# A gated decode block: the last V's joining ahead of eight late w_o steps, its copy on two engines, other pieces of the last transfer

## The chip, the cores and the metric

The kernel runs on one core of one Trainium2 chip. The core has TensorE (matmuls; PE in the profile, with its weight loads as PEld), VectorE (DVE), ScalarE (ACT), GpSimd (POOL) and SyncE (SP, which here issues nearly all transfers), and 16 DMA engines that bring data from HBM into SBUF. Matmul results stand in PSUM.

The metric is the device time of one execution in microseconds. The time before is 377.09 us, the median of 3 runs (376.98 to 377.14).

## The reference

One decode step of grouped-query attention on a cache, gated by a small bilinear network, all in float32:

```python
# B = 2, Sq = 1, D = 448, Hq = 16, Hkv = 8, Sk = 4096, Dh = 256, F = 1792
def A(x, k_cache, v_cache, wq, wo):
    q = (x @ wq).reshape(B, Sq, Hq, Dh).transpose(0, 2, 1, 3)
    k = repeat(k_cache, Hq // Hkv, axis=1)
    v = repeat(v_cache, Hq // Hkv, axis=1)
    p = softmax(einsum("bhqd,bhkd->bhqk", q, k) * Dh ** -0.5)
    o = einsum("bhqk,bhkd->bhqd", p, v)
    return o.transpose(0, 2, 1, 3).reshape(B, Sq, Hq * Dh) @ wo

def G(x, w_gate, w_up, w_down):
    return ((x @ w_gate) * (x @ w_up)) @ w_down

xn = layernorm(x)
out = x + A(xn, ...) * silu(G(xn, ...))
```

The caches are most of the data: 16 pairs of a batch row and a K/V head, each with 4 MB of K and 4 MB of V. With the weights some 158.5 MB are read once.

## The kernel before, in words

**Staging.** K and V of a pair stand in SBUF as tiles of 128 partitions by 8,192 float32 columns (`ROW`). The pool `ring` has two buffers of 16,384 columns. Each holds V of one pair and K of the next (`vk`), so a buffer is free again, and SyncE may issue the next transfer into it, when the scores on its K are done. Weights pass through one buffer, `slot`. The order of all transfers is a list written out by hand (`plan`, lines 82 to 90), and `issue(n)` (line 59) hands the next n of them to SyncE at places chosen in the code. An entry can have cuts: each piece between two cuts is a transfer of its own (lines 69 and 70), in the order of the columns, and its readers wait for that piece only.

The last two entries differ from the rest. `last0` holds K of pair 15 and V of pair 14, in two pieces. `last1` (line 90) holds V of pair 15 and behind it, under the name `wo2`, those chunks of w_o that are used last. Its cuts make six pieces: V's columns in 4,096, 3,072 and 1,024, then the chunks in groups of five, four and one.

**A pair.** `scores(i)` (line 231) multiplies q with K: 16 matmuls of 512 columns in four column groups of TensorE side by side. `softmax` (line 246) takes the maximum over the pair's four groups through two small TensorE transposes and the exponential on ScalarE, and VectorE transposes the result (`pT`). `over` (line 266) sums and inverts. `values(i, pT, o, lo, hi)` (line 274) multiplies with V: blocks e from lo to hi of 512 columns each, block e in column group e % 4; the four groups add up partial sums in one PSUM bank. Of 16 blocks, 0 to 3 begin the sums and 12 to 15 end them. In the profile each float32 matmul stands as two records.

**Joining.** ScalarE copies the partial sums to SBUF (`ob`), scaled by the inverse sum. `combine` (line 281), called the joining here, adds the four groups' parts with eight small matmuls against a matrix of ones and zeros (`add_blocks`), reading `ob` and writing the bank `cb`. `turn` (line 296) is a VectorE transpose of `cb` into `oT0`, `oT1` or `oT2`, the form in which TensorE takes it as weights. Both batch rows of a K/V head land in the same `oT` tile.

**Output projection.** w_o has 32 chunks of 128 rows by 448 columns, 224 KB each; chunk i belongs to K/V head i // 4. Chunks 0 to 15 need `oT0`, 16 to 27 need `oT1`, and 28 to 31 need `oT2`, which is complete only after the last V. `project` (line 302) multiplies chunk i in column group i % 4 into the bank `wide`; it runs for chunks 0 to 15 in the middle of the kernel and for 16 to `LATE` - 1 near the end (line 353). `lift` copies `wide` to SBUF and `spread` (line 201) adds up its four groups into the bank `acc`, 112 columns to a group.

The other chunks are the late steps. `project_last` (line 308) does one with four matmuls of 112 columns straight into `acc`. Their order, which is also their order in the transfer, is the list `THIRD` (line 28): ten of them, 22 to 26, then 28 to 31, then 27.

**The end.** Each engine works through its own instructions in the program's order. After line 353 stand: the softmax of pair 15; `values` of pair 14 (line 357); `spread`; the copy of pair 14 (line 361); blocks 0 to 7 of pair 15 into `o`, which takes the bank `wide` over (line 363); the joining and turn of pair 14; blocks 8 to 15; the copy of pair 15 on ScalarE (line 367); late steps 22 to 24; the joining and turn of pair 15 (lines 370 and 371); late steps 25, 26, 28 to 31 and 27. Then VectorE multiplies `acc` with the gate and adds x (lines 380 and 381), and the result is stored.

`wo` on the host (lines 415 to 417) is put in the order of chunks 0 to `LATE` - 1 followed by `THIRD`; the first `LATE` chunks are the transfer into `slot` that is issued with the pairs in the middle, the rest is appended to the last V.

Of the kernel before, what the change touches and what calls it, by code (L numbers as in the profile page):

```python
# [9 lines left out]
AF = mybir.ActivationFunctionType  # L10
OP = mybir.AluOpType
AX = mybir.AxisListType

B, D = 2, 448
# [8 lines left out]
ROW = 8192  # L23
SL = D // NT
NC = HKV * 4
EARLY = 16
LATE = 22
THIRD = [22, 23, 24, 25, 26, 28, 29, 30, 31, 27]
PART = 28 * FC
EXTRA = 4  # L30
SIDE = 16
# [8 lines left out]
def gated_decode_block(ctx: ExitStack, tc: tile.TileContext, x, first, vk, last0, last1, wq0, wq1, wqx, wo, wgu, wd, out):  # L40
    nc = tc.nc
# [7 lines left out]
    def bank(name="s", bufs=3):  # L49
        return psum.tile([128, 512], F32, name=name, bufs=bufs)  # L50
# [4 lines left out]
    LAST = N - B  # L55
# [3 lines left out]
    def issue(n=1):  # L59
        for names, src, cuts in todo[:n]:  # L60
            weight = names[0].startswith("w")
            if weight:
                t = slot.tile([128, PART], F32, name="slot", align_bytes=512)
            else:
                t = ring.tile([128, 2 * ROW], F32, name="ring", align_bytes=512)
            width = ROW if not weight else PART // len(names)
            for i, name in enumerate(names):
                loaded[name] = t[:, i * width:(i + 1) * width]
            for lo, hi in zip(cuts, cuts[1:]):
                nc.sync.dma_start(t[:, lo:hi], src[:, lo:hi])  # L70
            if names == ["wq1"]:
                at = src.shape[1]
                loaded["wqx"] = t[:, at:at + EXTRA * 512]
                nc.gpsimd.memset(loaded["wqx"][:64], 0.0)
                for a in range(2):
                    nc.sync.dma_start(loaded["wqx"][a * 32:a * 32 + SIDE], wqx[:, a])
        del todo[:n]

    def plan(names, src, cuts=None):
        todo.append((names.split(), src, cuts or [0, src.shape[1]]))  # L80
# [6 lines left out]
        if i in weights:  # L87
            plan(*weights[i])
    plan(f"k{LAST + 1} v{LAST}", last0, [0, ROW, 2 * ROW])
    plan(f"v{LAST + 1} wo2", last1, [0, 4096, 7168, *(ROW + i * D for i in (0, 5, 9, 10))])  # L90
    issue(3)


# [41 lines left out]
    oT1 = const.tile([128, 3, 2, REP, W], F32)  # L135
# [60 lines left out]
    def lift(ps):  # L196
        t = work.tile([128, D], F32, name="h")
        nc.scalar.copy(t, ps[:, :D])
        return t
# [66 lines left out]
    def over(p):  # L266

        pT, su, sm = p
        nc.vector.tensor_add(su[:, 2:3], su[:, 0:1], su[:, 1:2])  # L269
        nc.tensor.matmul(sm[:, 130:131], add_head.rearrange("p a r j -> p (a r j)"), su[:, 2:3], start=True, stop=True)  # L270
        nc.vector.reciprocal(su[:, 3:4], sm[:, 130:131])
        return pT, su[:, 3:4]

    def values(i, pT, o, lo=0, hi=KB):

        for e in range(lo, hi):
            h, t, at = e // 8, e % NT, e % 8 * 2 * W
            nc.tensor.matmul(o[W * t:W * (t + 1), :], pT[h][:, at:at + 2 * W:2],  # L278
                             loaded[f"v{i}"][:, e * 512:(e + 1) * 512], start=e < NT, stop=e >= KB - NT)

    def combine(ob, n):

        cb = bank("cb", 1)
        src = ob.rearrange("p s (e d c k) -> p s e d c k", e=2, d=2, c=NT)
        for e in range(2):
            for c in range(NT):
                nc.tensor.matmul(cb[W * c:W * (c + 1), :n * 64], add_blocks[:, e].rearrange("p r j -> p (r j)"),  # L287
                                 src[:, :n, e, :, c, :], start=e == 0, stop=e == 1)
        return cb
# [6 lines left out]
    def turn(oT, cb, g, b, n):  # L296
        nc.vector.transpose(oT[:, g:g + n, :, :, DUP * b:DUP * (b + 1)].rearrange("p g d r j -> p (g d) r j"), cb)

    def heads(oT, i, first):
        return oT[:, i // 4 - first, i % 2, i % 4 // 2]  # L300

    def project(oT, first, lo, hi):
        for i in range(lo, hi):
            t = i % NT
            nc.tensor.matmul(wide[W * t:W * (t + 1), :D], heads(oT, i, first),  # L305
                             loaded["wo"][:, i * D:(i + 1) * D], start=i < NT, stop=i >= LATE - NT)

    def project_last(oT, first, i):
        for n in range(NT):
            at = THIRD.index(i) * D + n * SL  # L310
            nc.tensor.matmul(acc[W * n:W * (n + 1), :SL], heads(oT, i, first), loaded["wo2"][:, at:at + SL],  # L311
                             start=False, stop=i == THIRD[-1])

    query(0)
    ob = work.tile([128, 8, 512], F32, name="ob", bufs=1)
    oT0 = const.tile([128, 4, 2, REP, W], F32)
    oT2 = const.tile([128, 1, 2, REP, W], F32)
# [3 lines left out]
    for i in range(LAST):  # L321
        g, b = divmod(i, B)
        o = bank("o", 1)
# [10 lines left out]
        if i == 7:  # L334
# [3 lines left out]
            ob = work.tile([128, 8, 512], F32, name="ob", bufs=1)  # L338
# [13 lines left out]
    ps = [over(p)]  # L352
    project(oT1, 4, EARLY, LATE)
    t = lift(wide)
    p = softmax(*ss)
    o = bank("o", 1)
# [5 lines left out]
    o = bank("wide", 1)  # L362
# [1 line left out]
    cb = combine(ob[:, 6:], 1)  # L364
    turn(oT2, cb[:, :64], 0, 0, 1)
    values(LAST + 1, ps[1][0], o, KB // 2, KB)
    nc.scalar.activation(ob[:, 7], o, AF.Copy, scale=ps[1][1])
    for i in range(LATE, 25):
        project_last(oT1, 4, i)
    cb = combine(ob[:, 7:], 1)  # L370
    turn(oT2, cb[:, :64], 0, 1, 1)
    for i in range(25, 27):
        project_last(oT1, 4, i)
    for i in range(28, 32):
        project_last(oT2, 7, i)
    project_last(oT1, 4, 27)

    r0 = work.tile([128, D], F32, name="h")[:, :SL]
    r1 = work.tile([128, D], F32, name="h")[:, :SL]
# [50 lines left out]
```

## Time and profile before

| what | value |
|---|---|
| median of 3 runs | 377.09 us (376.98 to 377.14) |
| the profiled execution | 378.13 us |
| its span, first to last instruction | 376.3 us |
| mean granted TensorE clock | 0.779 |
| TensorE busy | 203.2 us (54% of the span) |
| VectorE busy | 73.1 us (19%) |
| ScalarE busy | 40.1 us (11%) |
| read from HBM | 158.54 MB, 421 GB/s over the span |
| the hardware DMA queue | 97.7% of 16 engines' span |

Times in the profile are microseconds from the start of the span unless marked ns. A line of the chain of waits has a start, a duration and what it was spent on; "DMA ring<-last" there is the time from the issue of a transfer to its landing. A line of the timeline has the start, the duration, the engine, the line of the kernel, the operation, the tile written and the tiles read, the shapes and the number of records; in brackets stand the engine's idle time before it and what ended it. In a list of transfers the last number is the median time from issue to landing. A line of the windows has the window, its length, each engine's busy time with its count of records, the granted TensorE clock, the busy share of the DMA engines and the GB/s that they moved. A group of instructions has its total busy time and the mean ns of one.

### The profile page before, as it was taken

How to read it: one execution, taken by the hardware profiler on the slowest of the kernel's cores; microseconds unless marked ns; L12 is line 12 of the kernel's file. 1: busy time of each engine (PE TensorE's matmuls, PEld its weight loads, DVE VectorE, ACT ScalarE, POOL GpSimd, SP SyncE). 2: the span in 40 equal slices, each digit the busy share in tenths (PEclk: the TensorE clock that was granted, in tenths of full speed). 3: DMA queues.
4: the chain of work that ended last, by engine and by line, in shares of the span. 5: the costliest groups of instructions: out<-in, count | busy, mean ns of one | idle time of the engine just before them, and what ended most of it. 6: DMA issues, size and time to landing. Idle time of an engine off the chain costs nothing.

```text
span 376.3 us, 3394 instructions
## 1 busy us (share of the span) xinstructions
PE 203.2 (54%) x1470; PEld 62.6 (17%) x1470; DVE 73.1 (19%) x179; ACT 40.1 (11%) x88; POOL 3.1 (1%) x8
## 2 busy tenths in 40 slices
PE   1550648091853919558282758513636372829773
PEld 1110112020210202102120212101111111213223
DVE  4012040003040030300403041300213021212510
ACT  1001020001012020100101010100102011010300
POOL 1000000000001000000000000000000000000000
PEclk9987588778678667896778689885859596859996
DMA  8998999998989999999999999999999999999992
GB/s 339 438 491 383 420 453 439 441 446 384 488 383 441 446 411 476 439 432 399 439 447 446 413 415 447 435 439 446 439 418 434 446 439 404 434 415 444 408 421 100
DMA packets 4121, 158.74 MB, mean 422 GB/s; under 512 B 490, under 2 KB 620, under 8 KB 876
## 3 DMA queue, kind: packets, MB, share of 16 engines
q1 hardware_dynamic: 4104, 158.54, 97.7%
q8 instruction: 11, 0.18, 0.2%
q14 instruction: 2, 0.02, 0.0%
q10 hardware_dynamic: 4, 0.00, 0.0%
HBM read 158.54 MB, written 0.01 MB: 421 GB/s over the span
## 4 chain that ended last, share of the span: by engine, by line
DMA 79%; PE 19%; SPq 1%; issue 0%; DVE 0%
DMA ring<-vk 67%; PE o L278 11%; PE s L241 8%; DMA ring<-last 6%; DMA ring<-first 5%; PE acc L311 1%; SPq L70 1%; DVE h L380 0%; DVE h L381 0%
## 5 line engine op out<-in xcount | busy, mean ns | idle before, releaser
L278 PE MATMUL o<-ring,pT 128*32 128x512 f32 x480 | 82.0, 846 | 83.4 <-DMA ring<-vk 82.7
L242 DVE TENSOR_REDUCE m<-s 128x1 f32<-128x512 f32 x32 | 22.1, 691 | 206.5 <-PE s L241 206.4
L241 PE MATMUL s<-ring,qT 128*32 128x512 f32 x512 | 59.7, 607 | 4.2 <-DMA ring<-first 4.2
L278 PEld LDWEIGHTS o<-ring,pT 128*32 128x32 f32 x480 | 20.3, 149 | 136.4 <-issue 109.1
L260 ACT ACTIVATE p<-s,m 128x512 f32<-128x512 f32 x32 | 21.7, 683 | 90.9 <-DVE m L255 90.9
L328 ACT ACTIVATE ob<-o,su 128x512 f32<-128x512 f32 x14 | 9.6, 688 | 196.8 <-PE o L278 196.8
L270 PE MATMUL sm<-su,add_head 128*128 128x1 f32 x32 | 8.2, 325 | 38.2 <-DVE su L269 38.2
L262 DVE STREAM_TRANSPOSE pT<-p 128x512 f32<-128x512 f32 x32 | 22.1, 711 | 15.7 <-ACT p L260 15.7
L241 PEld LDWEIGHTS s<-ring,qT 128*32 128x32 f32 x512 | 17.4, 112 | 43.3 <-issue 39.2
L176 PE MATMUL s<-slot,xnT 128*32 128x448 f32 (+1 forms) x94 | 15.3, 782 | 4.3 <-DMA slot<-wq 3.6
L270 PEld LDWEIGHTS sm<-su,add_head 128*128 128x128 f32 x32 | 6.8, 265 | 40.4 <-DVE su L269 40.3
L249 PE MATMUL sm<-ident,m 128*1 128x128 f32 x16 | 4.3, 269 | 15.1 <-DVE m L247 15.1
L251 DVE TENSOR_REDUCE mx<-sm 1x128 f32<-1x512 f32 x16 | 10.9, 678 | 8.3 <-PE sm L249 8.3
L254 PE MATMUL sm<-one,mx 1*128 1x1 f32 x16 | 3.5, 218 | 12.4 <-DVE mx L251 12.4
L305 PE MATMUL wide<-slot,oT 128*32 128x448 f32 x44 | 6.3, 681 | 0.0
L260 ACT ACTIVATION_READ_ACCUMULATOR p<-s,m 128x1 f32 x32 | 6.3, 196 | 0.0
L249 PEld LDWEIGHTS sm<-ident,m 128*1 128x1 f32 x16 | 1.3, 79 | 28.8 <-issue 23.1
L287 PE MATMUL cb<-ob,add_blocks 128*32 128x64 f32 (+2 forms) x64 | 5.9, 491 | 0.0
L176 PEld LDWEIGHTS s<-slot,xnT 128*32 128x32 f32 x94 | 3.6, 141 | 13.2 <-issue 13.2
L278 PE MATMUL wide<-ring,pT 128*32 128x512 f32 x32 | 4.2, 599 | 2.2 <-DMA ring<-last 2.2
L222 PE MATMUL s<-slot,hT 128*32 128x448 f32 x28 | 5.1, 842 | 0.0
L188 DVE STREAM_TRANSPOSE qT<-s 128x256 f32<-128x256 f32 x4 | 1.6, 428 | 17.9 <-PE s L179 17.9
(69 smaller groups left out, 55.9 us busy)
## 6 DMA issues: line engine op xcount, KB each, us to landing
ring<-last SPq DMA_DIRECT2D x2, 4096.0 KB, 19.3
slot<-wgu SPq DMA_DIRECT2D x1, 6272.0 KB
slot<-wo SPq DMA_DIRECT2D x1, 4928.0 KB, 41.4
ring<-first SPq DMA_DIRECT2D x1, 4096.0 KB, 20.4
slot<-wq SPq DMA_DIRECT2D x1, 3584.0 KB, 11.2
slot<-wq SPq DMA_DIRECT2D x1, 3328.0 KB, 33.6
slot<-wd SPq DMA_DIRECT2D x1, 3136.0 KB, 37.7
ring<-last SPq DMA_DIRECT2D x1, 2048.0 KB, 15.6
```

The costliest lines, as they stand in the source:

```text
L176: nc.tensor.matmul(ps[W * c:W * (c + 1), :n], xnT[:, k, :], block(NT * k + c), start=k == 0, stop=False)
L241: nc.tensor.matmul(s[W * c:W * (c + 1), :], q[:, d], k[:, h, d, c, :], start=d == 0, stop=d == 1)
L242: nc.vector.tensor_reduce(m[:, h:h + 1], s, axis=AX.X, op=OP.max)
L249: nc.tensor.transpose(sm[:1, :128], m[:, 2:3], ident)
L251: nc.vector.tensor_reduce(mx, sm[:1, None, :128].rearrange("p o (c j) -> p o j c", c=NT).to_broadcast([1, NT, W, NT]), axis=AX.X, op=OP.max)
L260: nc.scalar.activation(p, ss[h], AF.Exp, bias=m[:, 3:4], scale=1.0 / 16, accum_out=su[:, h:h + 1])
L262: nc.vector.transpose(t, p)
L270: nc.tensor.matmul(sm[:, 130:131], add_head.rearrange("p a r j -> p (a r j)"), su[:, 2:3], start=True, stop=True)
L278: nc.tensor.matmul(o[W * t:W * (t + 1), :], pT[h][:, at:at + 2 * W:2], loaded[f"v{i}"][:, e * 512:(e + 1) * 512], start=e < NT, stop=e >= ...
L287: nc.tensor.matmul(cb[W * c:W * (c + 1), :n * 64], add_blocks[:, e].rearrange("p r j -> p (r j)"), src[:, :n, e, :, c, :], start=e == 0, s ...
L305: nc.tensor.matmul(wide[W * t:W * (t + 1), :D], heads(oT, i, first), loaded["wo"][:, i * D:(i + 1) * D], start=i < NT, stop=i >= LATE - NT)
L328: nc.scalar.activation(ob[:, b * 4 + g if g < 4 else b * 3 + g - 4], o, AF.Copy, scale=p[1])
```

## The change

Two more chunks of w_o, 22 and 23, go with the early w_o transfer and are multiplied by `project`. Eight late steps are left: 24 to 26, 28 to 31, 27. The last transfer is cut otherwise: V in 6,144 and 2,048 columns, the late steps in groups of three, three, one and one. The copy of pair 15 is shared: ScalarE scales and copies the first 256 columns, VectorE the other 256. The joining and turn of pair 15 stand ahead of all late steps.

```diff
-LATE = 22
-THIRD = [22, 23, 24, 25, 26, 28, 29, 30, 31, 27]
+LATE = 24
+THIRD = [24, 25, 26, 28, 29, 30, 31, 27]
...
-    plan(f"v{LAST + 1} wo2", last1, [0, 4096, 7168, *(ROW + i * D for i in (0, 5, 9, 10))])
+    plan(f"v{LAST + 1} wo2", last1, [0, 6144, *(ROW + i * D for i in (0, 3, 6, 7, 8))])
...
     values(LAST + 1, ps[1][0], o, KB // 2, KB)
-    nc.scalar.activation(ob[:, 7], o, AF.Copy, scale=ps[1][1])
-    for i in range(LATE, 25):
-        project_last(oT1, 4, i)
+    nc.scalar.activation(ob[:, 7, :256], o[:, :256], AF.Copy, scale=ps[1][1])
+    nc.vector.tensor_scalar(ob[:, 7, 256:], o[:, 256:], ps[1][1], None, op0=OP.mult)
     cb = combine(ob[:, 7:], 1)
     turn(oT2, cb[:, :64], 0, 1, 1)
-    for i in range(25, 27):
-        project_last(oT1, 4, i)
-    for i in range(28, 32):
-        project_last(oT2, 7, i)
-    project_last(oT1, 4, 27)
+    for i in THIRD:
+        project_last(*((oT2, 7) if i >= 28 else (oT1, 4)), i)
```

## The prediction

> **What bounds the kernel now.** I read the chain of waits first, by engine and then in order of time.
>
> ```profile
> DMA 79%; PE 19%; SPq 1%; issue 0%; DVE 0%
> ```
>
> ```profile
> 345.46 0.33 SPq L70
> 345.84 0.42 SPq L70
> ...
> 347.26 23.51 DMA ring<-last
> ...
> 370.91 2.13 PE acc L311 x40
> ```
>
> The kernel is a stream of transfers, and the chain leaves it only at 370.77 us (347.26 + 23.51), when the piece with w_o steps 28 to 31 lands. Behind that landing stand five late steps on TensorE (40 records, 2.13 us), then two VectorE operations and the store. Only this tail can change: the bytes are the same. The issues of the last pieces and their times to landing give the schedule of the tail.
>
> ```profile
> 347.73 1.12 SPq L70 DMA_DIRECT2D ring<-last  x1
> ```
>
> ```profile
> ring<-last SPq DMA_DIRECT2D x1, 2048.0 KB, 15.6
> ring<-last SPq DMA_DIRECT2D x1, 1536.0 KB, 18.9
> ...
> ring<-last SPq DMA_DIRECT2D x1, 224.0 KB, 23.6
> ```
>
> The 2,048 KB of V landed at 345.46 + 15.6 = 361.06, the next 1,536 KB at 345.84 + 18.9 = 364.74, steps 28 to 31 at 370.77, step 27 at 347.73 + 23.6 = 371.33. So 1,536 KB take 3.68 us, 0.54 us for the 224 KB of one step (the last piece: 0.56) and 1.23 us for 1,024 columns of V. What the engines do around this is in the timeline.
>
> ```profile
> 352.65 1.70 PE L305 MATMUL wide<-slot,oT 128*32 128x448 f32 x12
> 354.27 0.27 PE L249 MATMUL sm<-ident,m 128*1 128x128 f32 x1
> 355.32 0.22 PE L254 MATMUL sm<-one,mx 1*128 1x1 f32 x1 [0.77 <-DVE mx L251]
> 356.23 3.64 PE L278 MATMUL o<-ring,pT 128*32 128x512 f32 x32 [0.70 <-DMA ring<-last]
> 359.69 0.38 PE L203 MATMUL acc<-h,add_tiles 128*32 128x112 f32 x8
> 360.00 0.38 PE L270 MATMUL sm<-su,add_head 128*128 128x1 f32 x2
> 361.18 1.93 PE L278 MATMUL wide<-ring,pT 128*32 128x512 f32 x16 [0.80 <-DMA ring<-last]
> 362.89 0.43 PE L287 MATMUL cb<-ob,add_blocks 128*32 128x64 f32 x16
> ```
>
> ```profile
> 364.76 2.30 PE L278 MATMUL wide<-ring,pT 128*32 128x512 f32 x16 [1.43 <-DMA ring<-last]
> 366.00 0.15 PEld L278 LDWEIGHTS wide<-ring,pT 128*32 128x32 f32 x4 [0.24 <-DMA ring<-last]
> 367.11 0.69 ACT L367 ACTIVATE ob<-wide,su 128x512 f32<-128x512 f32 x1 [6.47 <-PE wide L278]
> 368.66 0.78 PE L311 MATMUL acc<-ring,oT 128*32 128x112 f32 x24 [1.60 <-DMA ring<-last]
> 369.26 0.41 PE L287 MATMUL cb<-ob,add_blocks 128*32 128x64 f32 x16
> 369.74 0.25 DVE L297 STREAM_TRANSPOSE oT<-cb 128x64 f32<-128x64 f32 x1 [6.10 <-PE cb L287]
> 370.91 2.10 PE L311 MATMUL acc<-ring,oT 128*32 128x112 f32 x40 [0.85 <-DMA ring<-last]
> ```
>
> Steps 22 to 24 waited for their piece until 368.66, 0.86 us after the copy of the last V (367.11 + 0.69), and the joining (L287) stood behind them. A late step costs 0.20 us there (368.66 to 369.26 for three), but 0.4 us in the last row (2.10 over five). The windows, cut at the clock's own borders, say why; after the window and its length come the busy us of PE, PEld, DVE, ACT and POOL, then the granted clock.
>
> ```profile
> 114.49:117.90 3.41, 1.64 (x20) 0.33 (x12) 0.00 (x0) 2.08 (x3) 1.80 (x1) 1.00 1.00 428
> 117.90:121.31 3.41, 0.00 (x0) 0.00 (x0) 0.27 (x1) 0.00 (x0) 0.00 (x0) 1.00 1.02 442
> 121.31:124.73 3.42, 2.45 (x12) 0.60 (x16) 0.00 (x0) 0.00 (x0) 0.00 (x0) 0.50 0.84 364
> 124.73:128.14 3.41, 3.41 (x20) 0.79 (x16) 0.00 (x0) 0.00 (x0) 0.00 (x0) 0.50 1.24 538
> ...
> 326.12:329.53 3.41, 1.54 (x14) 0.35 (x6) 1.65 (x4) 0.00 (x0) 0.00 (x0) 1.00 0.89 384
> 329.53:332.94 3.41, 0.61 (x3) 0.50 (x2) 1.75 (x5) 1.45 (x4) 0.00 (x0) 0.50 1.02 442
> ...
> 336.36:339.77 3.41, 2.80 (x16) 0.91 (x20) 0.00 (x0) 0.00 (x0) 0.00 (x0) 0.50 1.05 452
> 339.77:343.18 3.41, 3.41 (x36) 1.05 (x32) 0.00 (x0) 0.69 (x1) 0.00 (x0) 1.00 1.07 461
> ...
> 367.08:370.49 3.41, 1.39 (x56) 1.15 (x56) 0.25 (x1) 0.69 (x1) 0.00 (x0) 1.00 0.60 244
> 370.49:373.90 3.41, 2.10 (x40) 1.73 (x40) 0.55 (x2) 0.00 (x0) 0.00 (x0) 0.50 0.02 6
> ```
>
> The clock changes only on a grid of 3.413 us (114.49 to 370.49 is 75 of them). After a stretch with 1.54 us of TensorE or less the next one is granted 0.50; with 1.64 us it stays at 1.00. From 0.50 it rises after 2.80 us and doesn't after 2.45. The wait up to 368.66 left 1.39 us in its stretch, so the five steps behind the last landing ran at half clock.
>
> **The change part by part.** *Two w_o chunks move from the last transfer into the w_o one.* 448 KB pass earlier, so everything in the stream between moves back by 448 / 1,536 x 3.68 = 1.07 us, and the end stays at 371.33. On TensorE L305 gets two steps more, 1.70 / 6 = 0.28 us each, under the wait for the last but one V. That V's 32 records then run from 357.30 instead of 356.23, and the two groups behind them end at 361.45 instead of 360.38. Late steps fall from ten to eight.
>
> *V in 6,144 and 2,048 columns, late steps in 3, 3, 1, 1.* SP issues six transfers as before. Counted back from 371.33 at 0.56 for the last step and 0.54 for the others: step 31 lands at 370.77, 28 to 30 at 370.23, 24 to 26 at 368.6, the second V piece at 367.0, the first (2 x 1.23 earlier) at 364.5. TensorE can thus begin this V at 364.55 where it began at 361.18, and has no work from 361.45 on: 3.1 us idle.
>
> *The V itself at full clock.* Eight blocks take 1.71 us (361.18 to the next group at 362.89), so 364.55 + 1.71 = 366.26; the first joining, 0.25 (a place in the row, not its 0.43 with drain), 366.5; eight blocks, 368.2; drain, 368.45. The second piece (367.0) is there when its blocks begin at 367.4.
>
> *The shared copy.* Half-width copies aren't in the trace; the nearest rows bound them.
>
> ```profile
> L227 ACT ACTIVATE h<-s 128x112 f32<-128x112 f32 x1 | 0.3, 264 | 0.0
> ...
> L367 ACT ACTIVATE ob<-wide,su 128x512 f32<-128x512 f32 x1 | 0.7, 688 | 6.5 <-PE wide L278 6.5
> ```
>
> ```profile
> L215 DVE TENSOR_TENSOR h<-s,h 128x448 f32<-128x448 f32 x1 | 0.6, 625 | 8.7 <-PE s L179 8.7
> ...
> L380 DVE TENSOR_TENSOR h<-acc,gate 128x112 f32<-128x112 f32 x1 | 0.3, 275 | 3.1 <-PE acc L311 3.1
> ```
>
> On a straight line between widths, 256 columns take 264 + 144/400 x 424 = 417 ns on ScalarE and 275 + 144/336 x 350 = 425 ns on VectorE. In the built program's order the VectorE half waits for ScalarE's semaphore, not only for TensorE's. So the halves follow each other: 0.42 + 0.43 and 0.06 between them, 0.91 us where the whole copy takes 0.69; were they side by side, 0.43. I take 0.91; 0.43 to 1.0 is the range. The second joining waits for both, and all eight late steps stand behind it on TensorE (24 to 26 will have landed at 368.6 and are held until 369.7); the two last VectorE operations wait for them.
>
> The Trainium skill ("PSUM — Partial Sum Buffer", section on bank collisions) says that two engines may not touch one bank in the same 32 partitions at once, even two readers. That speaks against a gain from sharing, as the built order does; no row here shows it.
>
> *The tail.* Copies from 368.5 to 369.4, joining from 369.47, transpose by 369.47 + 0.41 + 0.04 + 0.25 = 370.2. Steps 24 to 26 from 369.7 to 370.3 (0.20 each), 28 to 30 (landed and turned) to 370.9, 31 to 371.1. Step 27 waits for its landing, 371.33, and 0.14 until TensorE begins (as 370.77 to 370.91); its 8 records take about 0.38 (0.20 and drain): the steps end at 371.85 against 373.04. Counted by work alone they would end near 371.6, so 0.25 us of slack swallows most of the errors above. The stretches here hold over 2 us of TensorE, so the clock stays full. Sum: 1.2 us less.
>
> The profiled execution took 378.13 us, its span 376.3; the median of the runs is 377.09, 1.04 below it. I take the same saving off the median, 375.9, and add 0.1, since nearly every unknown above can only lengthen it: **376.0 us**.
>
> **The rivals.** The idle time from 361.45 to 364.55 is where they lie, because the grid's place against the kernel decides. With a border at x between 359.9 and 360.4, the stretch from x holds under 1.54 us of work, the clock halves at x + 3.41 (before 364.55), and the next stretch holds 2.2 to 2.7 us, too little to rise. *Two stretches at half clock*: V runs at half speed from 364.55 to about 370.35 and loses 2.9 us; copies, joining and eight steps follow, ending near 374.5: +1.5, **378.6 us**, slower. It decides from the point where V's blocks stand at half clock at 367.1 still. For it: the recorded grid has a border at 360.25. Against: only 0.5 of 3.41 us of places do it, and 2.53 us there lies between the 2.45 that didn't rise and the 2.80 that did.
>
> *One stretch at half clock*: with the border between 358.7 and 359.3 (or the recorded one, if 2.53 us suffices) 1.7 us are lost; V ends at 370.15, copies at 371.1, joining and eight steps (0.25 + 1.6 + 0.26) at 373.2: +0.2, **377.3 us**.
>
> In the other places, some 70%, nothing is lost. In half of all places the clock halves at 357.0 to 358.7 already, since TensorE idles before the last but one V too; its blocks then end up to 1.7 us later, at 363.1, still ahead of 364.55, and that fills the gap.
>
> The Trainium skill ("TensorE: Matmul & The Clock Gate", Part 1) has the window at 3,413 ns and free-running, and lets the clock fall after an idle one. The grid agrees. By its rule a gap of 3.1 us would never halve the clock, and both rivals would give 376.0; the rows (1.39 and 1.54 us busy, and it fell) say otherwise.
>
> *The old tail was already fast in the timed runs*: if their grid stood so that the last five steps ran at full clock, they ended at 370.91 + 1.0 + 0.2 = 372.1, and the change gains 0.25 us: **376.8 us**. For it: the profiled execution is 1.04 us above the median, about what half clock costs the five steps. Against: profiling alone may cost that.
>
> **How the numbers follow.** Forecast 0.47; fast old tail 0.12; one stretch 0.15; two stretches 0.21; the rest 0.05. The forecast's own range is 375.6 to 376.5. The range is 375.5 (sharing side by side, all steps on time) to 378.9 (two stretches and a copy of 1.0). A measurement here can tell 0.2%, 0.75 us, from no change: faster is below 376.34, slower above 377.84. Faster 0.43 (nearly all of the forecast), same 0.29 (fast old tail, one stretch, the forecast's slow end), slower 0.28 (two stretches, the rest and some of one stretch).
>
> **What would show it.** Right: V's first block at about 364.5, the last piece at 371.3, ScalarE's half of 0.42 us ending before VectorE's begins, the second joining ahead of all late steps near 369.5, one step (8 records) behind the last landing, granted clock 1.00 from 364 to the end. Wrong: the copies overlapping; a landing order other than counted; TensorE still busy with V after 368.5 at 0.50, which would make it one of the slower rivals.

## The result, and the profile after

| | median | lowest to highest | runs |
|---|---|---|---|
| before | 377.19 us | 376.87 to 378.20 | 22 |
| after | 378.28 us | 376.73 to 379.57 | 22 |

The ratio is 1.0024, with a 95% interval from 1.0013 to 1.0035: the change made the kernel slower, by 0.24% as that ratio has it and by 1.09 us from median to median.

The spread is as telling as the median. The 22 runs after fall into three groups: 4 from 376.73 to 377.16, 15 from 377.88 to 378.71, 3 from 379.40 to 379.57. Before, 18 of 22 lie between 376.87 and 377.39 and 4 between 377.88 and 378.20. Over all 106 runs of the kernel before in this study 28 are in the upper group, 26%.

The profiled execution of the changed kernel took 378.10 us (span 376.2) and so belongs to the middle group, the usual one. That of before, 378.13 us, belonged to the upper and rarer one. Side by side the two profiled executions are equal, and the loss shows only once it is seen which of their groups they come from.

First the shares and the end of the chain of waits after, in order of time (start, duration, what).

```profile
DMA 77%; PE 21%; issue 0%; DVE 0%; ACT 0%; SPq 0%
```

```profile
346.76 17.51 DMA ring<-last
364.27 0.14 issue
364.41 2.68 PE wide L278 x16
367.09 0.43 PE cb L287 x16
367.52 2.48 PE wide L278 x16
370.02 0.48 ACT ob L367
370.53 0.49 DVE ob L368
371.06 0.32 PE cb L287 x8
371.38 1.58 PE acc L311 x64
```

Before, the chain left the transfers at 370.77 us, 2.3 us ahead of the last two VectorE operations. Now it leaves them at 364.27, with the landing of V's 6,144 columns, and runs 8.7 us through TensorE, ScalarE, VectorE and TensorE again. No later landing is in it: the last step's piece landed at about 349.03 + 22.0 = 371.0 us, while TensorE worked on the late steps until 372.96.

```profile
349.03 1.04 SPq L70 DMA_DIRECT2D ring<-last  x1
```

```profile
ring<-last SPq DMA_DIRECT2D x2, 224.0 KB, 22.0
```

The two groups of V's blocks took 2.68 and 2.48 us in the chain. Eight blocks had taken 1.93 at full clock before, the drain (the tail of the last matmul) included. The windows at the clock's borders (busy us of PE, PEld, DVE, ACT, POOL, then the granted clock) show it:

```profile
355.20:358.62 3.42, 2.46 (x26) 0.76 (x22) 1.51 (x4) 1.98 (x5) 0.00 (x0) 1.00 0.98 422
358.62:362.03 3.41, 2.56 (x30) 0.94 (x22) 0.92 (x4) 0.69 (x1) 0.00 (x0) 1.00 0.96 413
362.03:365.44 3.41, 1.03 (x12) 0.50 (x16) 0.00 (x0) 0.00 (x0) 0.00 (x0) 1.00 0.95 400
365.44:368.86 3.42, 3.42 (x35) 1.26 (x28) 0.25 (x1) 0.00 (x0) 0.00 (x0) 0.50 0.90 365
368.86:372.27 3.41, 2.62 (x74) 1.49 (x70) 0.73 (x2) 0.47 (x1) 0.00 (x0) 1.00 0.21 75
```

TensorE's wait for the 6,144 columns left the stretch from 362.03 with 1.03 us of work. The next stretch was granted half clock, and it is the one in which V is multiplied. One full stretch at half clock costs 1.7 us. Timeline rows after around it:

```profile
353.94 1.71 PE L305 MATMUL wide<-slot,oT 128*32 128x448 f32 x16
...
357.03 3.64 PE L278 MATMUL o<-ring,pT 128*32 128x512 f32 x32 [0.19 <-DMA ring<-last]
...
360.80 0.38 PE L270 MATMUL sm<-su,add_head 128*128 128x1 f32 x2
...
364.41 2.68 PE L278 MATMUL wide<-ring,pT 128*32 128x512 f32 x16 [3.23 <-DMA ring<-last]
...
370.02 0.47 ACT L367 ACTIVATE ob<-wide,su 128x256 f32<-128x256 f32 x1 [8.59 <-PE wide L278]
370.53 0.48 DVE L368 TENSOR_SCALAR ob<-wide,su 128x256 f32<-128x256 f32 x1 [2.72 <-ACT ob L367]
```

TensorE is idle for 3.23 us ahead of V. L305 starts at 353.94, 1.29 us later than before (352.65), and not where the prediction left it. The two half copies stand one after the other, as the built order had it: 0.47, 0.04 and 0.48 us.

### The profile page after: what moved, and what is told of

The parts are those of the page before. It is cut to its first block, busy times and chain, and to the rows that moved or that the text cites. A ratio compares the mean times of both kernels' runs of the same rounds, so it can differ in the third digit from the quotient of the medians.

```text
span 376.2 us, 3371 instructions
## 1 busy us (share of the span) xinstructions
PE 208.0 (55%) x1458; PEld 62.8 (17%) x1458; DVE 73.6 (20%) x180; ACT 39.9 (11%) x88; POOL 3.0 (1%) x8
## 4 chain that ended last, share of the span: by engine, by line
DMA 77%; PE 21%; issue 0%; DVE 0%; ACT 0%; SPq 0%
DMA ring<-vk 67%; PE o L278 11%; PE s L241 8%; DMA ring<-first 5%; DMA ring<-last 5%; PE wide L278 1%; PE acc L311 0%; PE cb L287 0%; DVE ob L368 0%; ACT ob L367 0%; SPq L70 0%; DVE h L376 0%; DVE h L377 0%
## 5 line engine op out<-in xcount | busy, mean ns | idle before, releaser
L278 PE MATMUL o<-ring,pT 128*32 128x512 f32 x480 | 83.0, 854 | 79.2 <-DMA ring<-vk 79.0
L241 PE MATMUL s<-ring,qT 128*32 128x512 f32 x512 | 60.9, 618 | 3.3 <-DMA ring<-first 3.3
L176 PE MATMUL s<-slot,xnT 128*32 128x448 f32 (+1 forms) x94 | 17.2, 871 | 5.5 <-DMA slot<-wq 3.6
L254 PE MATMUL sm<-one,mx 1*128 1x1 f32 x16 | 3.5, 218 | 12.4 <-DVE mx L251 12.4
L305 PE MATMUL wide<-slot,oT 128*32 128x448 f32 x48 | 7.2, 759 | 0.0
L278 PE MATMUL wide<-ring,pT 128*32 128x512 f32 x32 | 5.4, 797 | 3.2 <-DMA ring<-last 3.2
L271 DVE RECIPROCAL su<-sm 128x1 f32<-128x1 f32 x16 | 2.7, 169 | 11.2 <-PE sm L270 11.2
```

What stands on the lines that cost most here:

```text
L176: nc.tensor.matmul(ps[W * c:W * (c + 1), :n], xnT[:, k, :], block(NT * k + c), start=k == 0, stop=False)
L241: nc.tensor.matmul(s[W * c:W * (c + 1), :], q[:, d], k[:, h, d, c, :], start=d == 0, stop=d == 1)
```

## The experiments

The theory after the result: the wait for the larger first piece of V lets the clock fall under V's blocks. I call it the clock theory. Its rivals put the loss on the order (eight steps behind the joining) or on the copy in two halves, at whatever clock. Beside each experiment the kernel before was run on the same chip.

**V in the old pieces.**

```diff
-    plan(f"v{LAST + 1} wo2", last1, [0, 6144, *(ROW + i * D for i in (0, 3, 6, 7, 8))])
+    plan(f"v{LAST + 1} wo2", last1, [0, 4096, 7168, *(ROW + i * D for i in (0, 3, 6, 7, 8))])
```

> The changed kernel with V again in 4,096, 3,072 and 1,024 columns, all else as changed. Clock theory (the wait of 3.2 us before the 6,144 columns lets the clock fall to 0.50 under V's blocks): V starts about 3 us earlier, no stretch falls under 1.5 us of TensorE, granted clock 1.00 through the tail, most runs near 376.8 us, spread under 0.7 us. Rival (the order is at fault: eight late steps behind the joining and a copy in two halves one after the other): the joining still holds back all late steps, so the median stays near 378.3 us.

Measured: 377.00 us median, 376.79 to 377.12 in 11 runs; the kernel before 377.15. Both upper groups are gone, with order and shared copy in place. The end of its chain of waits:

```profile
348.57 21.35 DMA ring<-last
369.92 0.14 issue
370.06 0.97 PE acc L311 x32
371.03 0.03 issue
371.06 0.44 PE acc L311 x8
```

The chain is back on a landing of the late steps' pieces, with the last five steps behind it (x32 and x8, two records to a matmul). This speaks against both rivals, but it also moves V's start, so it can't tell the clock from the late start.

**Work put into the wait.**

```diff
     ps.append(over(p))
+    w = bank()
+    for e in range(8):
+        nc.tensor.matmul(w[W * (e % NT):W * (e % NT + 1), :], ps[0][0][0][:, :2 * W:2],
+                         loaded[f"v{LAST}"][:, e * 512:(e + 1) * 512], start=True, stop=True)
```

> The changed kernel with eight more matmuls on the V before (their result is used by nobody) in TensorE's wait for the 6,144 columns, 1.7 us at full clock. Clock theory: the stretch that held 1.03 us of TensorE holds 2.7, the clock stays at 1.00, V's blocks take 3.7 us instead of 5.6 and most runs come to about 376.8 us, though TensorE has more to do. Rival (V starts too late and the chain behind it is too long, at whatever clock): the start of V doesn't move and the median stays near 378.3 us.

Measured: 376.78 us median, 376.68 to 377.37 in 11 runs; before 377.15, the ratio 0.9989 (0.9980 to 0.9998). TensorE does more, V starts almost where it did, and the kernel is 1.5 us faster than the changed one by the medians. Its timeline and its windows:

```profile
361.49 1.93 PE L362 MATMUL s<-ring,pT 128*32 128x512 f32 x16
364.28 1.93 PE L278 MATMUL wide<-ring,pT 128*32 128x512 f32 x16 [0.86 <-DMA ring<-last]
365.99 0.43 PE L287 MATMUL cb<-ob,add_blocks 128*32 128x64 f32 x16
366.21 1.93 PE L278 MATMUL wide<-ring,pT 128*32 128x512 f32 x16
...
369.38 2.03 PE L311 MATMUL acc<-ring,oT 128*32 128x112 f32 x64
```

```profile
360.04:363.45 3.41, 3.38 (x38) 1.09 (x30) 0.17 (x1) 0.69 (x1) 0.00 (x0) 1.00 0.92 394
363.45:366.87 3.42, 2.59 (x40) 1.19 (x44) 0.25 (x1) 0.00 (x0) 0.00 (x0) 1.00 1.00 416
```

L362 is the filling. V starts at 364.28 against 364.41, but its blocks run at 1.00 and are done at 368.14 (366.21 + 1.93) instead of 370.0. With V 0.13 us earlier and the clock full, the loss of 1.09 us is gone, and 0.4 us more. The profile alone would not carry this: its stretch from 360.04 would have held some 1.45 us without the filling (3.38 less 1.93), about the limit. The timed runs do: none of 11 lies above 377.37, where 18 of 22 of the changed kernel did.

**Less of it.** The same with four matmuls, `range(4)`.

> The changed kernel with four filling matmuls instead of eight: TensorE's idle time before V is about 2.0 to 2.3 us instead of 3.2. Clock theory with the limit of 1.54 to 1.64 us of work in a stretch of 3.41: a stretch falls short when more than 1.8 us of the idle time lie in it, which is so for (idle time less 0.3) / 3.41 of the places of the clock's grid, 85% at 3.2 us, 0 at 1.5 us, and some 50 to 60% here. So about half of the runs near 378.2 us and half near 376.8 us. Rival (any gap, or a threshold near empty stretches): all runs in one of the two groups.

Measured: 8 of 11 runs from 376.56 to 377.11, 3 from 378.28 to 378.83, median 377.08. So both groups occur, as the theory has it and the rival has not, but 27% in the upper one, not 50 to 60%. The one profiled run suggests why the count was off: the V before began at 357.80 there, not 357.03, so the idle time was 1.8 us, just about the limit. Whether it was as short in the other runs is not shown.

```profile
357.80 3.64 PE L278 MATMUL o<-ring,pT 128*32 128x512 f32 x32
...
361.87 1.07 PE L362 MATMUL s<-ring,pT 128*32 128x512 f32 x8
364.73 1.92 PE L278 MATMUL wide<-ring,pT 128*32 128x512 f32 x16 [1.79 <-DMA ring<-last]
```

**The copy whole on ScalarE.**

```diff
-    nc.scalar.activation(ob[:, 7, :256], o[:, :256], AF.Copy, scale=ps[1][1])
-    nc.vector.tensor_scalar(ob[:, 7, 256:], o[:, 256:], ps[1][1], None, op0=OP.mult)
+    nc.scalar.activation(ob[:, 7], o, AF.Copy, scale=ps[1][1])
```

> The changed kernel with the copy of the last V whole on ScalarE again. If the two halves one after the other are the main cost, the median falls to 377.2 us or less. Clock theory: only what the copies took beyond 0.69 us comes back, 1.0 (0.47 + 0.03 + 0.48) less 0.69, so 0.3 us: median near 378.0 us with the same three groups of runs near 376.6, 378.0 and 379.2 us.

Measured: 377.80 us median; one run at 376.61, nine from 377.49 to 377.98, one at 378.95. The three groups stay, so the copy is not the cause; without sharing the middle group is 0.48 us lower by the medians, more than the 0.3 expected. Two more profiled runs of this kernel were to find the rest. The first:

> The changed kernel with the whole copy once more, for a profile of a run near 377.8 us. The medians say that sharing costs 0.48 us (378.28 against 377.80); the copies alone explain 0.3. If the rest is in the same chain: from the start of the copy to the last late step 0.45 to 0.5 us less than the 2.95 us in the changed kernel's profile (370.02 to 372.97). If it lies elsewhere: only 0.2 to 0.3 us less, and V's blocks end earlier by the rest.

It came out at 376.69 us, at full clock, and so says nothing of the 0.48 us. It did show that the limit is not sharp: its stretch from 362.45 held 1.45 us of TensorE, and the next stayed at 1.00.

```profile
364.42 1.93 PE L278 MATMUL wide<-ring,pT 128*32 128x512 f32 x16 [3.22 <-DMA ring<-last]
```

```profile
362.45:365.87 3.42, 1.45 (x16) 0.66 (x20) 0.00 (x0) 0.00 (x0) 0.00 (x0) 1.00 0.96 404
365.87:369.28 3.41, 2.61 (x52) 0.89 (x45) 0.25 (x1) 0.69 (x1) 0.00 (x0) 1.00 0.86 343
```

The second:

> As the look before, which fell among the runs at full clock: the changed kernel with the whole copy, for a profile near 377.8 us. If the 0.48 us lie in the chain behind V: 2.95 us from the start of the copy to the last late step become 2.45 to 2.5. If not: 2.65 to 2.75 us, and V's blocks end earlier by the rest.

At 377.74 us it fell into the middle group. Timeline and the windows around V:

```profile
364.28 3.44 PE L278 MATMUL wide<-ring,pT 128*32 128x512 f32 x16 [3.21 <-DMA ring<-last]
367.42 0.70 PE L287 MATMUL cb<-ob,add_blocks 128*32 128x64 f32 x16
367.85 1.99 PE L278 MATMUL wide<-ring,pT 128*32 128x512 f32 x16
...
369.90 0.69 ACT L367 ACTIVATE ob<-wide,su 128x512 f32<-128x512 f32 x1 [8.57 <-PE wide L278]
370.64 0.43 PE L287 MATMUL cb<-ob,add_blocks 128*32 128x64 f32 x16 [0.80 <-ACT ob L367]
370.88 1.72 PE L311 MATMUL acc<-ring,oT 128*32 128x112 f32 x64
...
372.67 0.27 DVE L375 TENSOR_TENSOR h<-acc,gate 128x112 f32<-128x112 f32 x1 [1.29 <-PE acc L311]
```

```profile
361.13:364.55 3.42, 0.27 (x4) 0.19 (x8) 0.15 (x1) 0.20 (x1) 0.00 (x0) 1.00 0.92 391
364.55:367.96 3.41, 3.41 (x36) 1.35 (x32) 0.00 (x0) 0.00 (x0) 0.00 (x0) 0.50 0.98 403
```

These two runs of one kernel are the closest comparison of the study. The gap ahead of V is the same (3.22 and 3.21 us), and V even starts 0.14 us earlier in the second. But the grid's borders lie elsewhere, at 362.45 and at 361.13, V runs at 1.00 in the first and at 0.50 in the second, and the second is 1.05 us slower.

From the copy to the VectorE operation behind the last step: 369.90 to 372.67, 2.77 us, against 370.02 to 372.99, 2.97 us, with sharing. So sharing costs 0.2 us in the chain. That is less than the copies' own 0.3, because the joining's first half already runs while VectorE copies. V's blocks started 0.13 us earlier in this run than in the profile of the changed kernel (364.28 against 364.41), with the landing. The remaining 0.15 us of the 0.48 is not explained; one profiled run of each can't say whether it is more than the scatter of the groups.

**The new pieces of V alone, in the kernel before.**

```diff
-    plan(f"v{LAST + 1} wo2", last1, [0, 4096, 7168, *(ROW + i * D for i in (0, 5, 9, 10))])
+    plan(f"v{LAST + 1} wo2", last1, [0, 6144, *(ROW + i * D for i in (0, 5, 9, 10))])
```

> The kernel before with V in 6,144 and 2,048 columns alone; ten late steps, three of them ahead of the joining, whole copy. Clock theory: the first V piece lands near 363.5 instead of 361.0 us, TensorE waits some 3.1 us, and V's blocks run at half clock in most runs; they end near 369.2 us instead of 367.1, and as steps 22 to 24 are there at once then, the end moves by only 0.2 to 0.5 us: median 377.4 to 377.7 us, some runs over 378.3 us. Rival (order and copy are at fault): the old order hides it, 377.1 us as before.

Measured: 377.18 us median, ten runs from 376.96 to 377.30 and one at 378.19; before 377.15. The clock did fall, as its windows say, and V ended 1.8 us later than before, yet the time stayed:

```profile
360.58:363.99 3.41, 0.69 (x8) 0.34 (x12) 0.00 (x0) 0.00 (x0) 0.00 (x0) 1.00 0.94 398
363.99:367.40 3.41, 3.41 (x36) 1.32 (x32) 0.25 (x1) 0.00 (x0) 0.00 (x0) 0.50 1.02 425
367.40:370.82 3.42, 3.08 (x84) 1.79 (x80) 0.25 (x1) 0.69 (x1) 0.00 (x0) 1.00 0.47 188
```

Expected were 377.4 to 377.7. The old order makes up for it in two ways: V's blocks end by 368.9 in this profile, steps 22 to 24 fill TensorE during the copy, and the busy stretch from 367.40 (3.08 us where the profile of before has 1.39) keeps the last five steps at full clock. So the pieces alone do not make the kernel slower: they need the rest of the change. That can be the new order, or the two w_o chunks moved ahead, by which V starts at 364.41 instead of 363.30; no run tells these two apart.

**The order alone, in the kernel before.**

```diff
-    for i in range(LATE, 25):
-        project_last(oT1, 4, i)
     cb = combine(ob[:, 7:], 1)
     turn(oT2, cb[:, :64], 0, 1, 1)
-    for i in range(25, 27):
+    for i in range(LATE, 27):
```

> The kernel before with the joining and transpose of the last V ahead of all ten late steps, nothing else. Clock theory: the copy ends near 367.8 us, ahead of the landing of steps 22 to 24 (368.6), so nothing is held back, five steps stay behind the landing of 28 to 31, and the median stays at 377.1 to 377.2 us with some runs near 378. Rival (the order costs by itself): slower by 0.3 us or more.

Measured: 377.25 us median (377.11 to 378.26, 3 of 11 runs above 378); before 377.26, the ratio 1.0003 (0.9993 to 1.0013). No cost by itself was seen. Its timeline:

```profile
367.79 0.43 PE L287 MATMUL cb<-ob,add_blocks 128*32 128x64 f32 x16 [0.79 <-ACT ob L367]
368.62 1.17 PE L311 MATMUL acc<-ring,oT 128*32 128x112 f32 x40 [0.40 <-DMA ring<-last]
370.86 1.17 PE L311 MATMUL acc<-ring,oT 128*32 128x112 f32 x40 [1.07 <-DMA ring<-last]
```

The joining is done before the first late steps land, so nothing is held back. The five last steps take 1.17 us here at full clock, where they took 2.10 in the profile of before.

**The upper group of before.** Four filling matmuls ahead of steps 22 to 24:

```diff
     nc.scalar.activation(ob[:, 7], o, AF.Copy, scale=ps[1][1])
+    w = bank()
+    for e in range(4):
+        nc.tensor.matmul(w[W * (e % NT):W * (e % NT + 1), :], ps[0][0][0][:, :2 * W:2],
+                         loaded[f"v{LAST}"][:, e * 512:(e + 1) * 512], start=True, stop=True)
     for i in range(LATE, 25):
```

> The kernel before with four more matmuls (0.85 us, result unused) in TensorE's wait ahead of steps 22 to 24, in the stretch that held 1.39 us in the profile of before. Clock theory: the runs of before near 378.0 us (9 of 33) are those whose five last steps ran at half clock, so they vanish and all runs lie at 376.9 to 377.3 us. Rival (they have another cause, for instance the transfers): a quarter of the runs stays near 378 us.

Measured: all 12 runs from 376.98 to 377.40, median 377.22; the kernel before beside it had 11 of 35 above 378. The ratio, 0.9993 (0.9985 to 1.0002), can't tell the medians apart, since the upper group is a minority, but that group is gone. With 28 of 106 as its share, 12 runs without it would be a chance of 3%. With the profile of before, which shows the five steps at 0.50, this makes the clock the likely cause of the upper group of before as well.

**Towards a faster kernel.** Two combinations of the above: the whole copy with the old pieces of V, and the whole copy with the eight filling matmuls.

> The changed kernel with V in 4,096, 3,072 and 1,024 columns and the copy whole on ScalarE: of the change, the eight late steps and their order remain. Clock theory: full clock, and the steps wait for their last piece, so the copy's 0.3 us lie in slack: 376.9 to 377.0 us, as with the shared copy and these cuts (377.0). If the shared copy costs on the path at full clock too: 0.2 to 0.5 us less, 376.5 to 376.8 us.

> The changed kernel with the eight filling matmuls and the copy whole on ScalarE. Clock theory: as with the filling alone, 376.7 to 376.8 us, since the last landing sets the end; a little fewer runs above 377. If the shared copy costs half a microsecond on the path at any clock: 376.3 us.

Measured: 377.02 us (376.82 to 377.37) and 376.79 us (376.54 to 377.27), the kernel before 377.29; ratios 0.9982 (0.9973 to 0.9992) and 0.9979 (0.9969 to 0.9988). At full clock the copy is in slack in both profiles: TensorE's last step waits for the landing of its piece and begins at 371.10 and 370.99 us. Their medians match the same kernels with the shared copy (377.00 and 376.78), but the kernel before was 0.14 us slower beside them than beside those, so a gain of that size is not excluded. Both are some 0.2% ahead of the kernel before.

## Why the prediction was wrong, by its own steps

The forecast was 376.0 us and faster; the measured median is 378.28, slower instead of faster, and within the range only because the slower rivals had widened it. Two steps failed. Of the 2.3 us between forecast and median some 1.5 are the fall of the clock (378.28 against 376.8 without it), 0.8 the base.

**"In half of all places the clock halves at 357.0 to 358.7 already."** This step made the gap before V harmless in some 70% of the grid's places. It moved the landings back by 1.07 us and left TensorE's work ahead of the last but one V at 352.65. But that work hangs on earlier landings of the same stream, which move as well. The last `vk` transfer landed at 336.84 before and at 337.66 after (start and duration in the chain, of before and of after):

```profile
307.37 29.47 DMA ring<-vk
```

```profile
308.67 28.99 DMA ring<-vk
```

This is not the chance of two runs: the landing lies between 336.54 and 336.94 in the four profiles in which chunks 22 and 23 still pass in the last transfer, and between 337.50 and 338.02 in the nine in which they pass earlier. L305 followed, to 353.94. (Of these 1.29 us part is scatter: it began anywhere from 352.65 to 353.98 in the four and from 353.42 to 354.97 in the nine.) The idle time that was to halve the clock early shrank from 0.70 us to 0.19, where the prediction had it grow, and the stretch from 355.20 held 2.46 us of work. By the prediction's own times it would have held some 1.5 us (0.22 of L254 and 1.3 of the V before), only just under the limit. In none of the nine profiles was a stretch between 350 us and the gap granted half clock. All that was left was the gap of 3.23 us. By the row with 1.54 us, 3.41 - 1.54 = 1.87 us of idle time in a stretch are enough, which holds for (3.23 + 3.41 - 2 x 1.87) / 3.41 = 85% of the places of the grid. 18 of 22 runs lay in the upper groups, 82%. The forecast gave its own case, no fall, 0.47; it came up in 4 of 22.

**"I take the same saving off the median."** The sum was made against a profiled execution with half clock in its last five steps, and that was not the usual state of before: 28 of 106 runs. The rival named it, a fast old tail with a gain of 0.25 us and 376.8 us, at a chance of 0.12. The two kernels with filling, 376.78 and 376.79 us, come to this number, and the four fastest runs of the changed kernel lie around it (376.73 to 377.16). So even without a fall the change was worth 0.3 to 0.5 us, not 1.2.

**The rivals' sizes.** One stretch at half clock was worked out as +0.2 us against the profile of before, an end of the steps at 373.2; the trace has 372.96. Against the profiled 378.13 that rival gives 378.3, and the median is 378.28. Taken off the median of before it became 377.3. So this rival had the mechanism right, and its chance (0.15 against 15 of 22 runs) and its base wrong. Two stretches, 378.6 and 0.21, would be the 3 of 22 runs at 379.4 to 379.6, since 378.6 plus the same 1.0 us of the base is 379.6. No run of that group was profiled, so this is an inference from the size.

**The schedule held.** V's first piece landed at 364.27 (predicted 364.5), the last step at 371.0 (371.33), all some 0.2 to 0.3 us early. One term was too large without consequence: the two steps more in L305 were put at 0.28 us each, and it took 1.71 us with them (16 records) and 1.70 without (12). The half copies took 0.47 and 0.48 us (0.42 and 0.43) and did not overlap; that order agrees with the Trainium skill ("PSUM — Partial Sum Buffer", bank collisions). At full clock, with filling, the joining began early enough for the last landing to set the end, as predicted.

**The limit of the clock held nearly.** Taken from two rows of before, 1.54 and 1.64 us, it gave nearly the right share of the runs. The Trainium skill ("TensorE: Matmul & The Clock Gate", Part 1) has the clock fall after an idle window; the stretch from 362.03 held 1.03 us of work, and it fell, so here the measurement decides.

## What to carry to other kernels

Where a kernel waits on transfers, a larger piece saves nothing if it makes TensorE wait longer in one go: look at each stretch of the clock's grid, and where a wait leaves one mostly idle (1.03 us of work in 3.41 here), the work behind the wait may run at half clock. Smaller pieces, or matmuls whose result nobody needs, can be worth more than the work that they add (376.78 against 378.28 us here). Before a sum is made against one profiled execution, see where it stands among the timed runs; and when a transfer is moved ahead in a stream, move back everything that hangs on what comes after, not only the landings under study.

## What the runs showed of the hardware that was not expected

- The clock's limits are bands, by the busy time that the profile counts. Over the thirteen profiles of this study, a stretch of 3.41 us at full clock with under 1.45 us of TensorE was always followed by half clock and one with over 1.63 never; between these both occur. From half clock, none rose after less than 2.6 us, and a few did not rise after 2.7 to 3.1.
- The place of the clock's grid differs from run to run of one kernel. In two profiled runs of the whole copy it made 1.05 us (376.69 and 377.74); the groups of the changed kernel lie 1.2 to 1.4 us apart. So a run of one kernel can differ from the next by more than this change is worth at full clock.
- The stream ended at 371.3 to 371.4 us in the profiles with all pieces as before (the kernel before, the order alone, its filling), and at 371.0 to 371.1 in the changed kernel, in the one with V's new pieces alone and in all experiments on the changed kernel but one (four filling matmuls, 371.4). What causes this was not tried.
